# Chunk 0's norm ahead of the identity casts, its products on VectorE, zero rows written early, 128-wide weights in the state update, new planner constants

## The chip, the cores and the metric

One core of one Trainium2 chip runs the whole kernel in one launch. The metric is the device time in microseconds (us) of one execution; the figure of a kernel is the median of its runs. Engines are named as TensorE (PE in the profile, PEld for its weight loads), VectorE (DVE), ScalarE (ACT), GpSimd (POOL) and SyncE (SP, which issues most transfers).

## The reference

Three stages follow each other, in float32, on a batch of 4 and a sequence of 768:

```
k_n = k / (|k| + 1e-6)                            # 8 heads of 48
for t: y[t] = q[t] @ state
       state += beta[t] * outer(k_n[t], v[t] - k_n[t] @ state)
x = y as (4, 768, 384)
u = x + ((x^T @ U @ V)^T);  x1 = u + relu(u @ w_ch1) @ w_ch2      # 384 -> 1536 -> 384
u = x1 + real(fft2(x1));    un = layer norm of u over 384
out = u + relu(un @ w2_ch1) @ w2_ch2
```

## The kernel before

**Tiles and stages.** The attention is cut into 24 chunks of 128 tokens (unit `u`; 6 per batch). A chunk goes through `s_front` (L705: norms of k and q, products with beta and the norms, each value split into a high and a low fp16 part), `s_turn` (L740: transposes KT, BT, K2; for chunk 0 on TensorE with the fp16 identity `id16`, for the others by transposing transfers), `s_prep_a` (L811: G = products of these, masked on VectorE), `s_split` (L851: G into GPh and GPl), `s_prep_b` and `s_prep_c` (L885, L951: the inverse of a triangular matrix by blocks) and `s_solve` (L1037: the solve and the state update, chunk after chunk). `mix_chunk` (L1010) collects x^T U. The first MLP runs over 8 blocks of 384 tokens (`s_mlp`, L1166: L1190 is the first layer, L1196 its high part `hh`, L1209 its low part `hl`, L1226 the second layer); `s_mix` (L1255) makes its input, `s_out1` (L1341) its output `x1d`, one tensor of 769 rows in DRAM for each batch. Row 768 is a zero row. The second part (`second`, L1636) takes the FFT through tables: `fold` (L1415) loads rows of `x1d` into `xq`, gathers mirrored rows with indirect transfers (`gather`, L1458, indices in the tile `rows`), adds and subtracts them into `pm`, and splits that into `fs` for the matmuls. Then follow the layer norm (`s_in`) and the second MLP.

**Who sets the order.** Each engine runs its instructions in the order in which they were issued. That order is made while the program is built, by `Weave` (L62): every stage is a generator (a stream) that yields the cost of its next step on each engine that may take it, or a mark to wait for; `Weave.run` (L139) picks the step with the lowest start time plus bias. `PR0` holds the biases of the attention's streams until the first tile of the mix, `PRICE0` the factors with which `pick` (L97) weighs engines against each other, `AGE0` and `EPS0` the weight of a chunk's age, `FILL` how far a stream of weight conversions may run into the next step of an engine, `UP` and `UE` how many chunks take a variant in which TensorE adds with an identity matmul. These are times of the plan; on the chip an engine waits for what its instruction reads. The first weights (float64 words to float32, three VectorE passes per 128x384 piece, L293, L296 and L300) are converted beside the attention's chunks.

**What the change touches.** `attn_pools` (L535) loads k and q of chunk 0, the identity `id32`, and casts it three times on VectorE (L569, L571, L573) before any stream runs. `row_scales` (L641) squares k and q on ScalarE (L647, L653), sums on VectorE (L649) and calls `norm` (L662: square root L667, reciprocal L670). `s_front` multiplies (through the helper `tt`, L251) and splits (`sub`, L589). `s_solve` starts with a matmul on `ids` (L1046), and its state update multiplies with 64-wide parts of `kb16` (helper `hmm`, matmul at L1055). `fft_pools` (L1394) loads `rows` (L1401), clears row 96 of `xq` (L1405) and writes it as the zero row of each `x1d` (L1407) before the second part's streams run.

With `u < UE` `s_split` doesn't subtract on GpSimd: TensorE subtracts the high part from G in PSUM with the matrix `idm` (minus identity), and ScalarE copies the rest out:

```
if u < UE:
    yield {"p": 440}
    nc.tensor.matmul(g32..., self.idm, gs..., start=False, stop=True, ...)
    yield {"a": _a(512, True)}
    nc.scalar.activation(out=gl, in_=g32, func=ACTF.Copy)
else:
    yield from self.sub(gl, g32, gs, 512)
```

Of the kernel before, what the change touches and what calls it, by code (L numbers as in the profile page):

```python
# [21 lines left out]
DM = 384  # L22
# [9 lines left out]
NR = 3  # L32
NQ = 2
NV = 2
AGE0 = -5
AGE = 16
EPS0 = -1085
FILL = 47
EPS = -309
UP = 13  # L40
UE = 0
NP = 27
GATE = 3
UA = 8
SPARE = 270
SPW = 120
PR0 = (-337, -112, -95, -78, -360, -173, -425, 225)
PR = (-41, -98, -140, -142, 118, 51, -956, -408)
ME = -78
MX = -401  # L50
MB = -515
MB0 = -564
P2 = (-467, -323, -887, -360, -372, -386, -1140, -392)
MP = 39
HB = -550
WB1 = -575
WB = -15
PRICE0 = {'p': 1.0, 'v': 1.45, 'a': 0.71, 'g': 0.38}
PRICE = {'p': 1.0, 'v': 0.29, 'a': 0.22, 'g': 0.14}
PRICE2 = {'p': 1.0, 'v': 283.18, 'a': 3.3, 'g': 1.14}  # L60
SC = 16.0
# [152 lines left out]
class Builder:  # L214
# [39 lines left out]
    def setup(self):  # L254
        nc, tc, ctx = self.nc, self.tc, self.ctx
        self.cst = ctx.enter_context(tc.tile_pool(name="cst", bufs=1))
        self.psm = ctx.enter_context(tc.tile_pool(name="psm", bufs=1, space=PSUM))
        self.psu = ctx.enter_context(tc.tile_pool(name="psu", bufs=1, space=PSUM))
        self.acc = ctx.enter_context(tc.tile_pool(name="acc", bufs=1, space=PSUM))
        self.dr = ctx.enter_context(tc.tile_pool(name="dr", bufs=1, space=bass.MemoryType.DRAM))  # L260
        self.wts = ctx.enter_context(tc.tile_pool(name="wts", bufs=1))
        self.keep = ctx.enter_context(tc.tile_pool(name="keep", bufs=1))
        c = self.cst
        few = c.tile([128, 58], F32, name="few")
        at = 0
# [12 lines left out]
        self.Vst = c.tile([96, S], F32R, name="Vst")  # L278
        self.ones = c.tile([128, 128], F32, name="ones")
        nc.gpsimd.memset(self.ones, 1.0)  # L280
        self.fsc = some(2, B)
        self.wsc1, self.unscale1 = some(2), some(1)
        self.wtot1, self.wss1 = some(2), some(2)
        self.usq, self.ucc = some(2, KD), some(2, 9)
        self.fsq, self.ftot = some(2 * KD), some(1)
# [249 lines left out]
    def attn_pools(self, ctx):  # L535
# [30 lines left out]
            return ts  # L566

        self.id16 = self.ap1.tile([128, 128], F16, name="id16")
        nc.vector.tensor_copy(out=self.id16, in_=self.id32)  # L569
        self.ids = self.ap1.tile([128, 128], F16, name="ids")  # L570
        nc.vector.tensor_scalar(out=self.ids, in0=self.id32, scalar1=SC, scalar2=None, op0=ALU.mult)  # L571
        self.idm = self.ap1.tile([128, 128], F16, name="idm")
        nc.vector.tensor_scalar(out=self.idm, in0=self.id32, scalar1=-1.0, scalar2=None, op0=ALU.mult)  # L573

        self.kq16 = zeros(NQ, [128, 2, H, 2, 64], "kq16")
        self.kb16r = zeros(NK, [128, H, 2, 64], "kb16")
# [9 lines left out]
        e = yield {"v" if psum else "w": _v(n, 4 if half else 1 if psum else 2), "a": _a(n, psum)}, mode  # L586
        self.copy(e, out, in_)

    def sub(self, out, in0, in1, n, mode="chain", op=ALU.subtract):  # L589
        e = yield {"w": _v(n), "g": _g(n)}, mode  # L590
        self.tt(e, out, in0, in1, op)

    def s_scales(self):
# [47 lines left out]
    def row_scales(self, u, b, c, kq, sq):  # L641

        nc = self.nc
        n = H + 1
        ss = self.ap2.tile([128, n], F32, tag="ssq", name="ssq", bufs=1)
        yield {"a": _a(DM)}
        nc.scalar.activation(out=sq, in_=kq[:, 0], func=ACTF.Square)  # L647
        yield {"v": _v(DM)}, "par"
        nc.vector.tensor_reduce(out=ss[:, 0:H], in_=sq, op=ALU.add, axis=AX.X)  # L649
        yield {"a": _a(DM) + 187}, "par"  # L650
        if u < UE:
            sq = self.ap2.tile([128, 512], F32, tag="g32", name="g32")[:, 0:DM].rearrange("p (h d) -> p h d", h=H)
# [52 lines left out]
    def s_front(self):  # L705
# [3 lines left out]
        for u, (b, c) in self.each():  # L709
            yield ("kq", u)  # L710
            kq = self.kq.pop(u)
            kb = self.ap2.tile([128, H, D], F32, tag="kb", name="kb", bufs=1)
            rn, rb, rq, sq1 = yield from self.row_scales(u, b, c, kq, kb)
            kq16, kb16 = self.kq16[u % NQ], self.kb16r[u % NK]
            if u >= NQ:
                yield ("tk", u - NQ)
            e = yield {"g": 830, "w": _v(DM)}, "par"
            self.tt(e, kb, kq[:, 0], rb[:, :, None].to_broadcast(bc), ALU.mult)
            e = yield {"a": 507, "w": 330}, "par"
            if e == "a":  # L720
                nc.scalar.activation(out=kq16[:, 1, :, 0, 0:D], in_=kq[:, 1], func=ACTF.Copy, scale=rq)
            else:
                nc.vector.tensor_scalar(out=kq16[:, 1, :, 0, 0:D], in0=kq[:, 1], scalar1=rq, scalar2=None, op0=ALU.mult)
            e = yield {"g": 830, "w": _v(DM)}, "chain"
            self.tt(e, kq[:, 0], kq[:, 0], rn[:, :, None].to_broadcast(bc), ALU.mult)
            if u >= NK:
                yield ("sol", u - NK)
            yield from self.cp(kb16[:, :, 0, 0:D], kb, DM)
            yield from self.cp(kq16[:, 0, :, 0, 0:D], kq[:, 0], DM)
            yield "join"  # L730
            yield from self.sub(kb16[:, :, 1, 0:D], kb, kb16[:, :, 0, 0:D], DM, "par")
            yield from self.sub(kq16[:, 0, :, 1, 0:D], kq[:, 0], kq16[:, 0, :, 0, 0:D], DM, "par")
            yield {"w": _v(DM)}, "par"
            nc.vector.scalar_tensor_tensor(out=kq16[:, 1, :, 1, 0:D], in0=kq[:, 1], scalar=rq, in1=kq16[:, 1, :, 0, 0:D],
                                           op0=ALU.mult, op1=ALU.subtract)
# [4 lines left out]
    def s_turn(self):  # L740

        nc = self.nc
        for u, _ in self.each():
# [293 lines left out]
    def s_solve(self):  # L1037
# [5 lines left out]
        St = S32 = None  # L1043
        flat = "p h d -> p (h d)"
        R = self.psr.tile([128, H, D], F32, name="res")
        nc.tensor.matmul(R, self.ids, self.X128[:, :, 0:D], start=True, stop=True, skip_group_check=True)  # L1046

        def f16t(tag):
# [31 lines left out]
        for u, (b, c) in self.each():  # L1080
# [44 lines left out]
            terms.append((lambda h: GPh[:, h, 128:256], Ul))  # L1125
            if c < NC - 1:
                ps = work()
                yield from hmm(ps, [(lambda h: kb16[:, h, 0, :], Uh), (lambda h: kb16[:, h, 1, :], Uh),
                                    (lambda h: kb16[:, h, 0, :], Ul)], m=64)
                yield {"v": _v(n)}  # L1130
                if c == 0:
                    S32 = self.ap2.tile([64, H, D], F32, tag="S32", name="S32", bufs=1)
                    nc.vector.tensor_scalar(out=S32, in0=ps[0:64], scalar1=1.0 / SC, scalar2=None, op0=ALU.mult)
                else:
                    nc.vector.scalar_tensor_tensor(out=S32, in0=ps[0:64], scalar=1.0 / SC, in1=S32, op0=ALU.mult, op1=ALU.add)
# [14 lines left out]
    def attention(self):  # L1150
# [2 lines left out]
        streams = [self.s_solve(), self.s_prep_c(), self.s_prep_b(0), self.s_prep_a(), self.s_split(), self.s_front(), self.s_turn(),  # L1153
                   self.s_scales()]
        streams = self.att = [Stream(x, (y, y)) for x, y in zip(streams, PR0)]
        streams = streams + [Stream(self.s_prep_b(1), (PR0[2], PR0[2])), Stream(self.s_turned(), (PR0[6], PR0[6])), Stream(self.s_load(), (0.0, 0.0)), Stream(self.s_values(), (0.0, 0.0)), Stream(self.s_mixed(), (MX, MX))]
        peaks, weights = self.weight_parts(self.w11, self.w12)
        parts = self.mix_parts() + peaks + weights
        self.loads = len(parts)
# [95 lines left out]
    def s_mix(self):  # L1255
# [4 lines left out]
        for n in range(B * S // TB):  # L1260
# [30 lines left out]
                self.wv.post("hst", b)  # L1291
            if n >= 2:
                yield ("out", 0, n - 2)
            if n == 1:
                yield ("conv", self.loads - 1)
            ut = self.keep.tile([128, 2, KD, TB], F32, tag=f"uh{n % 2}", name="u1")
# [97 lines left out]
    def fft_pools(self, ctx):  # L1394
# [2 lines left out]
        self.fp1 = ctx.enter_context(tc.tile_pool(name="fp1", bufs=1))  # L1397
        self.fp2 = ctx.enter_context(tc.tile_pool(name="fp2", bufs=2))
        self.tab = {nm: self.fp1.tile([128, 2, 2, w], F16, name=nm) for nm, w in TABS}
        self.rows = self.fp1.tile([128, KD * B + 4], mybir.dt.int32, name="rows")  # L1400
        nc.sync.dma_start(self.rows, self.crows)  # L1401
        self.xq = [self.fp1.tile([97, 4, DM], F32, name=f"xq{i}") for i in range(2)]
        for i, x in enumerate(self.xq):
            if i == 0:
                nc.gpsimd.memset(x[96:97], 0.0)  # L1405
                for x1 in self.x1d:
                    nc.sync.dma_start(x1[S:S + 1], x[96:97, 3, :])  # L1407

    def s_tables(self):
        for (nm, w), src in zip(TABS, self.ctab):  # L1410
# [4 lines left out]
    def fold(self, b):  # L1415
# [5 lines left out]
        for i, x in enumerate(self.xq):  # L1421
# [8 lines left out]
            for y in range(2):  # L1430
                yield from self.gather(b, x[0:96, 1 + y, :], KD * B + 2 * i + y)
            yield "join"
            pm = self.fp1.tile([97, 2, 2, 2 * NE], F32, tag="pm", name="pm")
            for y, op in enumerate((ALU.add, ALU.subtract)):
                e = yield {"w": _v(2 * DM), "g": _g(2 * DM)}, "par"
# [317 lines left out]
```

## Time and profile before

| | us |
|---|---|
| median of 3 runs | 1038.92 (1038.15 to 1038.94) |
| the profiled execution | 1041.91 |
| its span, first to last instruction | 1039.8 |
| TensorE busy | 913.1 (88%) |
| VectorE busy | 724.9 (70%) |
| ScalarE busy | 548.6 (53%) |
| GpSimd busy | 352.2 (34%) |
| mean granted TensorE clock | 0.939 of full speed |

The profile is of one execution. Busy times of an engine add up its instructions; a stage is read from its own stretch, since the attention (to about 575 us), the first MLP (from 211 us) and the second part (from 577 us) overlap and have different limits. A line of the timeline gives start, duration, engine, source line, what it writes and reads, and in brackets the idle time before it with what ended that.

### The profile page before, as it was taken

To read this page: it belongs to the slowest core of one execution; us is meant where nothing else is said; L and a number is where in the kernel's file an instruction comes from. 1 tells how busy PE (TensorE), PEld (TensorE's weight loads), DVE (VectorE), ACT (ScalarE), POOL (GpSimd) and SP (SyncE) were. 2 spreads that over 40 slices of the span, in tenths; PEclk is the share of its full clock that TensorE was granted. 3 is DMA by queue.
4 is the path that set the end of the run, shared out by engine and by line. 5 is a ranking of instruction groups with operands and counts; after the bars stand their busy time and mean duration, and the time that the engine had idled before them with its cause. 6 is when DMAs were issued, how large, how long until landed. Compare 5 with 4: busy or idle time off the path is not lost. (4 is left out here: it accounts for less than half of the span.)

```text
span 1039.8 us, 25511 instructions
## 1 busy us (share of the span) xinstructions
PE 913.1 (88%) x10282; PEld 622.6 (60%) x10282; DVE 724.9 (70%) x1664; ACT 548.6 (53%) x1358; POOL 352.2 (34%) x330
## 2 busy tenths in 40 slices
PE   3465777589999899999999879999999999999998
PEld 2344665356777666676676546655756665655655
DVE  6898889898898998998765367765735554444532
ACT  5665676767777766667655244447723232222221
POOL 3554244213444323454110360046555532012010
PEclk8575989589999999999999989999999999999999
DMA  6996677316756565543502546522211311202110
GB/s 189 224 219 163 160 183 174 78 39 146 152 133 162 105 151 112 142 109 79 114 25 70 164 105 192 130 87 71 35 54 50 95 28 54 69 24 61 58 34 23
DMA packets 158253, 110.87 MB, mean 107 GB/s; under 512 B 117484, under 2 KB 146424, under 8 KB 158136
## 3 DMA queue, kind: packets, MB, share of 16 engines
q1 hardware_dynamic: 155688, 102.01, 40.6%
q0 software_dynamic: 2448, 7.24, 2.5%
q8 instruction: 80, 1.31, 0.5%
q14 instruction: 37, 0.30, 0.1%
HBM read 55.63 MB, written 14.16 MB: 67 GB/s over the span
## 5 line engine op out<-in xcount | busy, mean ns | idle before, releaser
L1226 PE MATMUL acc<-w2s,hh 128*128 128x384 f16 x1152 | 281.8, 326 | 4.9 <-DVE u L1624 3.1
L1190 PEld LDWEIGHTS <-w1s 128*128 128x128 f16 x1728 | 163.5, 98 | 114.5 <-issue 14.7
L1196 ACT ACTIVATE hh<-ps_h 128x384 f16<-128x384 f32 x192 | 93.7, 488 | 205.6 <-PE ps_h L1190 201.8
L251 POOL TENSOR_TENSOR GPl<-g,GPh 128x512 f16<-128x512 f32 x92 | 116.1, 1262 | 235.1 <-ACT GPh L244 174.2
L1209 DVE SCALAR_TENSOR_TENSOR hl<-ps_h,hh 128x384 f16<-128x384 f32 x147 | 81.6, 555 | 161.6 <-ACT hh L1196 155.8
L1226 PE MATMUL acc<-w2s,hl 128*128 128x384 f16 x576 | 188.1, 327 | 0.2 <-DVE hl L1209 0.2
L1190 PE MATMUL ps_h<-u,w1s 128*128 128x384 f16 x864 | 169.6, 329 | 11.9 <-DVE hl L1209 10.5
L1190 PE MATMUL ps_h<-uh,w1s 128*128 128x384 f16 x864 | 157.9, 327 | 0.0
L1226 PEld LDWEIGHTS <-hh 128*128 128x128 f16 x1152 | 106.2, 98 | 64.8 <-issue 8.0
L902 PEld LDWEIGHTS <-bd 128*128 128x128 f16 x1728 | 71.6, 99 | 45.7 <-issue 18.6
L1226 PEld LDWEIGHTS <-hl 128*128 128x128 f16 x576 | 56.2, 98 | 38.2 <-DVE hl L1209 0.6
L841 DVE TENSOR_TENSOR g<-ps_g,mask 128x512 f32<-128x512 f32 x96 | 65.6, 683 | 12.1 <-PE ps_g L835 11.0
L834 PE MATMUL ps_g<-KT,BT 128*128 128x256 f16 x192 | 54.0, 301 | 10.0 <-ACT t L993 5.0
L244 ACT ACTIVATE GPh<-g 128x512 f16<-128x512 f32 x75 | 47.0, 626 | 28.0 <-DVE g L841 27.3
L251 POOL TENSOR_TENSOR pair<-x1f,pair 128x384 f16<-128x384 f32 x24 | 22.2, 925 | 111.8 <-ACT pair L1594 106.8
L251 POOL TENSOR_TENSOR pm<-xq 97x768 f32<-97x768 f32 (+1 forms) x16 | 29.3, 1850 | 79.5 <-DMA xq<-x1d 72.1
L835 PE MATMUL ps_g<-K,BT 128*128 128x256 f16 x192 | 54.6, 305 | 1.9 <-DMA K<-KT 1.8
L1068 ACT ACTIVATE rh<-res 128x384 f16<-128x384 f32 x63 | 30.5, 484 | 20.0 <-PE res L1055 10.2
L902 PE MATMUL lanes<-R,bd 128*128 128x32 f16 x768 | 34.7, 179 | 4.5 <-ACT R L244 2.9
L882 DVE TENSOR_TENSOR bd<-Xc,mmask 128x1024 f16<-128x1024 f16 x48 | 34.2, 712 | 5.9 <-ACT Xc L936 5.5
L1055 PEld LDWEIGHTS <-GPh 128*128 128x128 f16 x768 | 30.2, 98 | 9.7 <-issue 6.7
L251 POOL TENSOR_TENSOR kb<-kq,rb 128x384 f32<-128x384 f32 x21 | 18.2, 867 | 50.8 <-DVE rb L658 10.9
(270 smaller groups left out, 1866.6 us busy)
## 6 DMA issues: line engine op xcount, KB each, us to landing
wst<-in_moe_w_ch_dram SPq DMA_DIRECT2D x51, 384.0 KB, 3.4
K<-KT SPq DMA_DIRECT2D x46, 256.0 KB, 3.9
kq<-in_k_dram SPq DMA_DIRECT2D x24, 192.0 KB, 3.8
kq<-in_q_dram SPq DMA_DIRECT2D x24, 192.0 KB, 4.2
vt<-in_v_dram SPq DMA_DIRECT2D x24, 192.0 KB, 2.9
xnd<-vt SPq DMA_DIRECT2D x24, 192.0 KB, 3.5
xn<-xnd SPq DMA_DIRECT2D x24, 192.0 KB, 3.0
x1d<-u SPq DMA_DIRECT2D x24, 192.0 KB, 1.9
```

The lines of the kernel that those rows point to most:

```text
L244: self.nc.scalar.activation(out=out, in_=in_, func=ACTF.Copy)
L251: (self.nc.vector if eng == "v" else self.nc.gpsimd).tensor_tensor(out=out, in0=in0, in1=in1, op=op)
L834: nc.tensor.matmul(o, BT[:, h, :], KT[:, :, h, :], start=i == 0, stop=False, skip_group_check=True)
L835: nc.tensor.matmul(o, BT[:, h, :], K2[:, :, h, :], start=False, stop=True, skip_group_check=True)
L841: nc.vector.tensor_tensor(out=g32.rearrange("p i (a t) -> p (i a) t", a=2), in0=ps.rearrange("p i (a t) -> p (i a) t", a=2), in1=self.mask ...
L882: self.nc.vector.tensor_tensor(out=dst.rearrange("p h (j c) -> p h j c", j=n), in0=x, in1=mask[:, None, :, :].to_broadcast(shape), op=ALU. ...
L902: nc.tensor.matmul(ps[:, h, :], lhs[:, h, :], rhs[:, h, :], start=plus is None, stop=plus is None or h == H - 1)
L1068: nc.scalar.activation(out=t, in_=R, func=ACTF.Copy, scale=-1.0 / SC)
L1190: nc.tensor.matmul(ps[:, i, :], w[:, k, fs], u[x][:, k, :], start=(m == 0), stop=(m == 3 * KD - 1))
L1196: nc.scalar.activation(out=hh, in_=ps, func=ACTF.Relu, scale=1.0 if wi else 1.0 - 2.0 ** -11)
L1209: nc.vector.scalar_tensor_tensor(out=hl, in0=ps, scalar=0.0, in1=hh, op0=ALU.max, op1=ALU.subtract)
L1226: nc.tensor.matmul(acc, h[:, ds_], w, start=(f == 0 and j == 0), stop=(f == KF - 1 and j == 2))
```

## The change

Three casts of the identity become a stream, `s_unit`, that waits until chunk 0's norm is done; the solve and chunk 0's transposes wait for it. Chunk 0's two products and two splits may run on VectorE alone, and the second square of chunk 0 is written to a block of `bd[3]` (of the next chunks, below `UE`, to a `g32` tile). The row table and a 12x32 zero tile are placed in the pool that lives from the start; the table's load and the four zero-row writes are issued in `s_mix` at n = 2. In the state update the weights are 128 wide (but for the last one), so that rows 64 to 127 of the product's tile receive values that nothing reads. A mark `gd` with offset `GD` = 0 is waited for before `pm`. The planner's constants of the first part change.

```diff
-AGE0 = -5
+AGE0 = 6
+GD = 0.0
-EPS0 = -1085
-FILL = 47
+EPS0 = -1190
+FILL = 148
-UP = 13
-UE = 0
+UP = 11
+UE = 4
-PR0 = (-337, -112, -95, -78, -360, -173, -425, 225)
+PR0 = (-226, -196, -174, -118, -335, -164, -241, 81)
-MB0 = -564
+MB0 = -441
-WB = -15
-PRICE0 = {'p': 1.0, 'v': 1.45, 'a': 0.71, 'g': 0.38}
+WB = -18
+PRICE0 = {'p': 1.0, 'v': 1.45, 'a': 0.24, 'g': 0.14}
...
+        self.rows = c.tile([128, KD * B + 4], mybir.dt.int32, name="rows")
+        self.zero = c.tile([12, 32], F32, name="zero")
+        nc.gpsimd.memset(self.zero, 0.0)
...
-        nc.vector.tensor_copy(out=self.id16, in_=self.id32)
-        nc.vector.tensor_scalar(out=self.ids, in0=self.id32, scalar1=SC, ...)
-        nc.vector.tensor_scalar(out=self.idm, in0=self.id32, scalar1=-1.0, ...)
...
-        if u < UE:
+        if u == 0:
+            sq = self.bd[3].rearrange(...).bitcast(F32)[:, 0:DM].rearrange(...)
+        elif u < UE:
...
             rn, rb, rq, sq1 = yield from self.row_scales(u, b, c, kq, kb)
+            if u == 0:
+                self.wv.post("scaled")
-            e = yield {"g": 830, "w": _v(DM)}, "par"
+            e = yield {"g": 830, "w": _v(DM)} if u else {"w": _v(DM)}, "par"
             self.tt(e, kb, kq[:, 0], rb[:, :, None].to_broadcast(bc), ALU.mult)
...
-            e = yield {"g": 830, "w": _v(DM)}, "chain"
+            e = yield {"g": 830, "w": _v(DM)} if u else {"w": _v(DM)}, "chain"
             self.tt(e, kq[:, 0], kq[:, 0], rn[:, :, None].to_broadcast(bc), ALU.mult)
...
+            yield from self.sub(kb16[:, :, 1, 0:D], kb, kb16[:, :, 0, 0:D], DM, "par", fast=u == 0)
+            yield from self.sub(kq16[:, 0, :, 1, 0:D], kq[:, 0], kq16[:, 0, :, 0, 0:D], DM, "par", fast=u == 0)
...
             if u == 0:
+                yield ("unit",)
...
+    def s_unit(self):
+        yield ("scaled",)
+        for t, x in ((self.id16, 1.0), (self.ids, SC), (self.idm, -1.0)):
+            yield {"v": 210.0}, "par"
+            self.nc.vector.tensor_scalar(out=t, in0=self.id32, scalar1=x, scalar2=None, op0=ALU.mult)
+        self.wv.post("unit")
...
         R = self.psr.tile([128, H, D], F32, name="res")
+        yield ("unit",)
         nc.tensor.matmul(R, self.ids, self.X128[:, :, 0:D], ...)
...
-                yield from hmm(ps, [(lambda h: kb16[:, h, 0, :], Uh), (lambda h: kb16[:, h, 1, :], Uh),
-                                    (lambda h: kb16[:, h, 0, :], Ul)], m=64)
+                yield self.pe(3 * H, 48, 64)
+                kf = kb16.rearrange("p h s d -> p (h s d)")
+                for i, (y, x) in enumerate(((0, Uh), (1, Uh), (0, Ul))):
+                    for h in range(H):
+                        z = 64 * (2 * h + y)
+                        z1 = min(z + 128, 128 * H)
+                        nc.tensor.matmul(ps[0:z1 - z, h, :], kf[:, z:z1], x[:, h, :], ...)
...
+            if n == 2:
+                self.nc.sync.dma_start(self.rows, self.crows)
+                for x1 in self.x1d:
+                    self.nc.sync.dma_start(x1[S:S + 1].rearrange("o (a c) -> (o a) c", a=12), self.zero)
...
-        self.rows = self.fp1.tile([128, KD * B + 4], mybir.dt.int32, name="rows")
-        nc.sync.dma_start(self.rows, self.crows)
...
-                for x1 in self.x1d:
-                    nc.sync.dma_start(x1[S:S + 1], x[96:97, 3, :])
...
+            self.wv.post("gd", b, i)
+            self.wv.mark["gd", b, i] += GD
+            yield ("gd", b, i)
             pm = self.fp1.tile([97, 2, 2, 2 * NE], F32, tag="pm", name="pm")
```

## Rows read from the trace of the kernel before

**Rows 1.** Busy time by stretch: engines (instructions), granted clock, DMA share, GB/s.

```profile
core 0: us, PE busy (x) PEld busy (x) DVE busy (x) ACT busy (x) POOL busy (x), PEclk, DMA share, GB/s
...
20.00:40.00 20.00, 8.97 (x82) 5.49 (x80) 18.20 (x42) 10.83 (x29) 11.57 (x12) 0.51 0.88 228
...
120.00:200.00 80.00, 52.02 (x965) 41.55 (x964) 69.47 (x160) 55.94 (x139) 32.96 (x32) 0.84 0.67 157
...
300.00:400.00 100.00, 95.53 (x1514) 70.08 (x1513) 91.47 (x206) 71.31 (x186) 37.57 (x34) 1.00 0.56 130
...
800.00:900.00 100.00, 99.07 (x682) 63.98 (x681) 52.92 (x137) 29.51 (x69) 32.11 (x30) 1.00 0.22 62
```

**Rows 2.** Timeline of TensorE: the first matmuls of the first MLP.

```profile
210.80 1.13 PE L1190 MATMUL ps_h<-u,w1s 128*128 128x384 f16 x3
```

**Rows 3.** Waits of TensorE, 560 to 1040 us: total us, times, longest us.

```profile
PE ps_h L1190 <- DVE hl L1209: 10.5, 4, 8.1
```

**Rows 4.** Timeline of single engines from 577 us (start, us), and a piece of the chain.

```profile
579.12 1.14 SPq L1407 DMA_DIRECT2D x1d<-xq  x4
...
583.43 1.14 POOL L1461 DMA_INDIRECT xq<-x1d,rows  x1 [4.66 <-DMA xq<-x1d]
...
585.43 0.43 SPq L1412 DMA_DIRECT2D sd<-in_sd_dram  x1
...
592.50 3.71 POOL L251 TENSOR_TENSOR pm<-xq 97x768 f32<-97x768 f32 x2 [6.71 <-DMA xq<-x1d]
...
600.49 0.94 ACT L1451 ACTIVATE fs<-pm,few 97x772 f16<-97x772 f32 x1 [8.96 <-POOL pm L251]
...
603.48 3.04 PE L1190 MATMUL ps_h<-u,w1s 128*128 128x384 f16 x9 [8.15 <-DVE hl L1209]
...
608.44 1.46 PE ps_h L1190 x9
...
757.25 0.91 POOL L1461 DMA_INDIRECT xq<-x1d,rows  x1 [0.30 <-issue]
761.21 3.59 POOL L251 TENSOR_TENSOR pm<-xq 97x768 f32<-97x768 f32 x2 [3.05 <-issue]
```

**Rows 5.** Timeline, 5 to 14 us: chunk 0's norm, products, splits and transposes.

```profile
5.42 0.21 ACT L675 ACTIVATE n_h<-n_s 128x9 f32<-128x9 f32 x1
6.73 0.23 DVE L569 CAST id<-id 128x128 f16<-128x128 f32 x1 [2.33 <-DMA id<-in_cident_dram]
...
7.15 0.21 DVE L670 RECIPROCAL n_t<-n_s 128x9 f32<-128x9 f32 x1
...
8.45 0.82 POOL L251 TENSOR_TENSOR kb<-kq,rb 128x384 f32<-128x384 f32 x1 [5.62 <-DMA wst<-in_moe_V_dram]
...
11.80 1.25 POOL L251 TENSOR_TENSOR kq<-kq,kq 128x384 f16<-128x384 f32 x1
...
13.11 1.03 PE L767 MATMUL ps_t<-id,kq 128*128 128x128 f16 x8 [5.45 <-POOL kq L251]
```

**Rows 6.** Groups by line, 0 to 125 us: busy us, mean ns | idle before.

```profile
L841 DVE TENSOR_TENSOR g<-ps_g,mask 128x512 f32<-128x512 f32 x22 | 15.0, 683 | 2.7 <-PE ps_g L835 2.3 <-POOL GPl L251 0.2
...
L293 DVE TENSOR_SCALAR wfp<-wst 128x384 uint32<-128x384 uint32 (+2 forms) x23 | 12.5, 545 | 1.3 <-DMA wst<-in_moe_U_dram 0.6 <-ACT UU L328 0.4
...
L244 ACT ACTIVATE GPh<-g 128x512 f16<-128x512 f32 x21 | 13.1, 626 | 9.8 <-DVE g L841 9.8
...
L251 POOL TENSOR_TENSOR GPl<-g,GPh 128x512 f16<-128x512 f32 x21 | 25.0, 1192 | 14.5 <-ACT GPh L244 14.4
```

**Rows 7.** Timeline of TensorE, 62 to 65 us: the state update and the output of chunk 0.

```profile
62.55 0.66 PE L1055 MATMUL ps_s<-Uh,kb 128*64 128x48 f16 x16 [0.53 <-DVE Ul L1121]
63.05 0.41 PE L1055 MATMUL ps_s<-Ul,kb 128*64 128x48 f16 x8
...
64.10 0.36 PE L1055 MATMUL ps_s<-Uh,GPh 128*128 128x48 f16 x8
64.31 0.36 PE L1055 MATMUL ps_s<-Uh,GPl 128*128 128x48 f16 x8
```

More of the change, by code (lines that the diff above doesn't have):

```diff
@@ L34 @@
 NV = 2
-AGE0 = -5
+AGE0 = 6
 AGE = 16
-EPS0 = -1085
-FILL = 47
+GD = 0.0
+TUNE = ("GD",)
+EPS0 = -1190
+FILL = 148
 EPS = -309
-UP = 13
-UE = 0
+UP = 11
+UE = 4
 NP = 27
@@ L568, in attn_pools @@
         self.id16 = self.ap1.tile([128, 128], F16, name="id16")
-        nc.vector.tensor_copy(out=self.id16, in_=self.id32)
         self.ids = self.ap1.tile([128, 128], F16, name="ids")
-        nc.vector.tensor_scalar(out=self.ids, in0=self.id32, scalar1=SC, scalar2=None, op0=ALU.mult)
         self.idm = self.ap1.tile([128, 128], F16, name="idm")
-        nc.vector.tensor_scalar(out=self.idm, in0=self.id32, scalar1=-1.0, scalar2=None, op0=ALU.mult)
         self.kq16 = zeros(NQ, [128, 2, H, 2, 64], "kq16")
@@ L587, in cp, with sub @@
         self.copy(e, out, in_)
-    def sub(self, out, in0, in1, n, mode="chain", op=ALU.subtract):
-        e = yield {"w": _v(n), "g": _g(n)}, mode
+    def sub(self, out, in0, in1, n, mode="chain", op=ALU.subtract, fast=False):
+        e = yield {"w": _v(n)} if fast else {"w": _v(n), "g": _g(n)}, mode
         self.tt(e, out, in0, in1, op)
@@ L650, in row_scales @@
         yield {"a": _a(DM) + 187}, "par"
-        if u < UE:
+        if u == 0:
+            sq = self.bd[3].rearrange("p h c -> p (h c)").bitcast(F32)[:, 0:DM].rearrange("p (h d) -> p h d", h=H)
+        elif u < UE:
             sq = self.ap2.tile([128, 512], F32, tag="g32", name="g32")[:, 0:DM].rearrange("p (h d) -> p h d", h=H)
@@ L730, in s_front @@
             yield "join"
-            yield from self.sub(kb16[:, :, 1, 0:D], kb, kb16[:, :, 0, 0:D], DM, "par")
-            yield from self.sub(kq16[:, 0, :, 1, 0:D], kq[:, 0], kq16[:, 0, :, 0, 0:D], DM, "par")
+            yield from self.sub(kb16[:, :, 1, 0:D], kb, kb16[:, :, 0, 0:D], DM, "par", fast=u == 0)
+            yield from self.sub(kq16[:, 0, :, 1, 0:D], kq[:, 0], kq16[:, 0, :, 0, 0:D], DM, "par", fast=u == 0)
             yield {"w": _v(DM)}, "par"
@@ L1127, in s_solve @@
                 ps = work()
-                yield from hmm(ps, [(lambda h: kb16[:, h, 0, :], Uh), (lambda h: kb16[:, h, 1, :], Uh),
-                                    (lambda h: kb16[:, h, 0, :], Ul)], m=64)
+                yield self.pe(3 * H, 48, 64)
[4 more added lines that the diff above has]
+                        z1 = min(z + 128, 128 * H)
+                        nc.tensor.matmul(ps[0:z1 - z, h, :], kf[:, z:z1], x[:, h, :], start=i == 0 and h == 0,
+                                         stop=i == 2 and h == H - 1, skip_group_check=True)
                 yield {"v": _v(n)}
@@ L1155, in attention @@
         streams = self.att = [Stream(x, (y, y)) for x, y in zip(streams, PR0)]
-        streams = streams + [Stream(self.s_prep_b(1), (PR0[2], PR0[2])), Stream(self.s_turned(), (PR0[6], PR0[6])), Stream(self.s_load(), (0.0, 0.0)), Stream(self.s_values(), (0.0, 0.0)), Stream(self.s_mixed(), (MX, MX))]
+        streams = streams + [Stream(self.s_prep_b(1), (PR0[2], PR0[2])), Stream(self.s_turned(), (PR0[6], PR0[6])), Stream(self.s_unit(), (0.0, 0.0)), Stream(self.s_load(), (0.0, 0.0)), Stream(self.s_values(), (0.0, 0.0)), Stream(self.s_mixed(), (MX, MX))]
         peaks, weights = self.weight_parts(self.w11, self.w12)
```

## The prediction

> **What bounds the kernel now.** I read the busy time by stage first, then what TensorE waited for late in the span, then the order of time at the two places that the change touches. The stages [rows 1] show two regimes. From 20 to 200 us TensorE is busy well under 70% of the time while VectorE is at 91% (18.20 of 20) and 87% (69.47 of 80), the transfers take 0.88 of the DMA engines at first, and the granted clock is 0.51 at first, which is the 1.2 GHz level for nearly all of that stretch. From about 300 us TensorE is the bound: 95.53 of 100 us, later 99.07 of 100, at a clock of 1.00. The first matmul of the first MLP stands at 210.80 us [rows 2]. So a microsecond counts in three ways: the dense regime beginning earlier, TensorE doing less in it, and a hole in it closing.
>
> The only large hole late in the span is one wait: of four waits of the first MLP layer for `hl` that sum to 10.5 us, one takes 8.1 us [rows 3]. Its cause is in [rows 4]. The fold of batch 0 (the start of the second part) gathers rows of `x1d` with indirect transfers on GpSimd. The first gather starts at 583.43, after GpSimd stood idle for 4.66 us behind a transfer. The row puts that down to a load of `xq`, but the gather doesn't touch what that load writes; it does read the tensor into which four writes of zero rows were issued on SyncE from 579.12 on, and I take those as the cause. `pm` on GpSimd starts only at 592.50; ScalarE's `fs`, queued ahead of the MLP's `hh`, waits 8.96 us for it until 600.49; then VectorE's `fs`, then `hl`; TensorE resumes at 603.48 after 8.15 us. Its first nine matmuls take 3.04 us where nine take 1.46 a little later, twice as long, as at the low one of the two clocks.
>
> **The change part by part.** Durations are of the profiled execution (1041.91 us, span 1039.8), which is 2.99 us above the median of the runs, 1038.92. Savings are taken off the median.
>
> 1. *Fold: zero rows and row table written in the first part.* Removed ahead of the fold: one load of the row table and four tiny writes on SyncE, and the gather's wait for them. GpSimd was free at 583.43 - 4.66 = 578.77, so two gathers can be out by 578.77 + 2 x 0.91 and the gap between, say 581.2, instead of 592.50 - 6.71 = 585.79. In a later fold the second gather ends at 757.25 + 0.91 = 758.16 and `pm` starts at 761.21, 3.05 us on [rows 4]; here it took 6.71 because loads of the FFT tables were issued up to 585.43 + 0.43 among them. So `pm` starts between 584.3 and 587.9, 8.2 to 4.6 us earlier. `hl` must still wait for its own conversions in VectorE's queue, so some stall stays. I take 5.5 us of the 8.15. Lower end 0 (the gathers still land behind the tables); upper end 8.15 + (3.04 - 1.46) = 9.7 us, if the clock never falls. What is late next is ScalarE's `fs` against `hh`, by a smaller amount. The five DMAs now issue in the first part at n = 2 of the mix stage, on SyncE, ahead of that tile's later transposes. I cost them at nothing: the writes of before took SyncE 1.14 us, and in that part of the run VectorE and TensorE set the pace, not the queue; uncovered it is about 1.2 us once. The new planner mark before `pm` adds no instruction: 0.
>
> 2. *Chunk 0's opening.* ScalarE's last result for the norm was under way at 5.42, but VectorE stood at the identity's cast, which waited 2.33 us for the load and ran at 6.73; the norm's reciprocal came at 7.15 [rows 5]. Moved behind the norm: 7.15 - 5.42 = 1.7 us. The two products and two splits took GpSimd from 8.45 to 11.80 + 1.25 = 13.05, passes of 0.82 to 1.25 us; a 128x384 pass on VectorE takes 0.55 [rows 6], so four take 2.2 and, with ScalarE's casts between, about 2.9: 1.7 us less. Against this the three casts (6.73 to 7.15, 0.42 us) now stand in VectorE's queue ahead of splits or converted weights, and VectorE takes over 2.2 us. Who waits: the transposes, which need the cast identity and began at 13.11 behind GpSimd's last split. Net 1.7 + 1.7 - 0.4 = 3.0 us at that point. But the stage behind it has VectorE at 91% and DMA at 0.88, so not all of it arrives at 210.8: I take 2.0, ends 0 and 3.4. The first square's own scratch removes a wait on ScalarE, yet the same reduction still feeds the square root: 0, at most one 0.55 us pass.
>
> 3. *State update with 128-wide weights.* The rows of the solve [rows 7] give the step: 16 products with 64-wide `kb` take 63.05 - 62.55 = 0.50 us, 31 ns each; 8 with 128-wide `GPh` take 64.31 - 64.10 = 0.21 us, 26 ns each. 23 of a chunk's 24 become 128 wide: 23 x 5 = 0.12 us; 20 chunks have one: 2.4 us, of which 15 chunks (1.8 us) lie after 210.8. The extra output rows are not read.
>
> 4. *UE 0 to 4, UP 13 to 11.* For four chunks the low part of G (16 of the 1192 ns passes on GpSimd [rows 6]) becomes an identity matmul and a ScalarE copy in PSUM. TensorE has room there [rows 1]; the new cost is a wait in its queue for VectorE's mask and ScalarE's copy, 683 + 626 ns a pair. Covered by other chunks' matmuls: 0; uncovered, 16 x 1.31 = 21 us. For two chunks eight 256-column matmuls leave TensorE, and a VectorE sum takes the place of a copy. A 384-column matmul takes 1.46 / 9 = 0.16 us, so at most 8 x 0.16 = 1.3 us gained; VectorE takes on at most 8 x 0.55 us, in a stage where it is at 91% and TensorE at 96%. I take 0.2, and 2.0 for parts 3 and 4 together (ends 0 and 3.7).
>
> 5. *Planner constants* (prices, biases, ages, FILL 47 to 148) move order in the first 200 us and remove no instruction. No row shows the new order. FILL lets a weight conversion start up to 101 ns later into another engine step's slot; up to 125 us there are 23 x 3 such passes [rows 6], so at worst 69 x 0.101 = 7.0 us of delay; a gain can't be excluded either. I take 0.
>
> Sum: 5.5 + 2.0 + 2.0 = 9.5; 1038.9 - 9.5 = 1029.4, call it 1029.5 (of the profiled execution: 1032.4).
>
> **A rule that speaks against part 3.** The rows show the 128-wide weights at the shorter step. The Trainium skill, page TensorE: Matmul & The Clock Gate, section LDWEIGHTS, makes a load's time the number of columns over 1.2 (in ns), whatever the rows: an estimate by it is 53 ns for 64 columns and 107 for 128, and by it alone part 3 would cost 23 x 20 x 53 ns = 25 us rather than save 2.4. The trace disagrees for this type and shape: I go by its 26 against 31 ns.
>
> **The rivals.**
> - *A, the fold doesn't gain.* The gathers still land with the table loads, which also move up, and `pm` starts where it did. For it: 6.71 us from issue to `pm`. Against it: 4.66 us of GpSimd's wait has a named cause that goes. Only parts 2 to 4 remain: 1038.9 - 4.0 = 1034.9.
> - *B, the new order eats the gain.* Conversions squeezed ahead of the attention chain delay 210.8 by the full 7.0 us and swallow part 2: 1038.9 - 7.5 + 7.0 = 1038.4, no change. For it: VectorE at 91%. Against it: only passes on the chain count.
> - *C, slower: TensorE's queue in the first four chunks.* The identity matmuls wait in order for mask and copy, and the solve of these chunks comes later. Place: 20 to 120 us; price up to 21 us; it decides once more than 7.5 + 2.1 = 9.6 us of it stays uncovered. With two thirds, 14 us: 1038.9 - 7.5 + 14 = 1045.4. Against it: two banks alternate, and TensorE works only 8.97 of 20 us there.
> - *D, slower: wider weights load longer.* If the step grew with the columns, 31 ns more for 23 x 20 products is 14.3 us: 1038.9 - 7.5 + 14.3 = 1045.7. Against it: [rows 7]. By that rule of the Trainium skill's page, this is what would happen.
>
> **How the numbers follow.** Forecast 0.60, A 0.17, B 0.10, C 0.10, D 0.03. A measurement here can tell about 0.2%, 2.1 us. Faster holds forecast and A, 0.77; within 0.2% is B, 0.10; slower is C and D, 0.13. Low end: all upper ends at once, 9.7 + 3.4 + 3.7 = 16.8, give 1022.1; a gain by order may stand in for one of them, and 1 us is left for it: 1021. The high end takes in A and B with some of B's spread: 1040. Outside are C and D and a little at the bottom, under 2 in 10.
>
> **What would show it.** Right: the first gather within 1 us of GpSimd coming free and no transfer ahead of it; `pm` 4.6 us or more earlier against the end of attention; the 8.1 us wait under 3; the reciprocal under 6 us and the first transposes near 10; `kb` loads 128 wide at 26 ns; the first MLP matmul near 208. Wrong: that matmul later than 211, identity matmuls of `idm` with idle TensorE before them in the first 100 us, or `pm` again 9 us after the first gather, as now (592.50 - 583.43).

## The result and the profile after

The changed kernel takes 1027.22 us (median of 4 runs, 1024.69 to 1028.83) against 1038.54 us of the kernel before in the same session: a ratio of 0.9889, 95% interval 0.9873 to 0.9906, 11.5 us faster (9.8 to 13.2). The forecast was 1029.5. The two profiled executions lie 17.2 us apart (1041.91 and 1024.69), further than the medians: what two single profiles show is read for its place and cause, and sizes are taken from the medians and ratios.

Head of the page after:

```profile
span 1022.9 us, 25488 instructions
...
PE 914.5 (89%) x10293; PEld 623.0 (61%) x10293; DVE 716.4 (70%) x1650; ACT 562.7 (55%) x1391; POOL 330.4 (32%) x311
```

Busy time by stretch after, columns as in [rows 1]:

```profile
20.00:40.00 20.00, 10.78 (x110) 6.62 (x108) 17.56 (x41) 13.54 (x34) 7.10 (x8) 0.50 0.84 180
...
120.00:200.00 80.00, 55.04 (x957) 44.59 (x957) 70.35 (x157) 58.37 (x150) 29.33 (x27) 0.78 0.69 160
...
300.00:400.00 100.00, 91.06 (x1409) 65.13 (x1407) 85.12 (x191) 72.32 (x188) 37.72 (x33) 1.00 0.59 134
...
800.00:900.00 100.00, 99.27 (x654) 62.30 (x653) 49.47 (x134) 27.73 (x64) 25.49 (x25) 1.00 0.21 58
```

Against [rows 1] work has gone from GpSimd (11.57 to 7.10 us of the first stretch) to ScalarE (10.83 to 13.54) and TensorE (8.97 to 10.78). VectorE is as full as before, and the granted clock of the first stretch is still the 1.2 GHz level, 0.50. Up to 200 us TensorE has run 2119 matmuls, 1914 before, and so has less left from 300 us; the gain lies before 120 us, for from 120 to 200 us it runs 957 against 965, and its longer busy time there (55.04 us against 52.02) goes with a lower clock (0.78 against 0.84).

Timeline after, the opening and the first matmul of the first MLP (start, duration, engine, line):

```profile
3.73 0.52 ACT L657 ACTIVATE bd<-kq 128x384 f32<-128x384 f32 x1
...
4.77 0.21 DVE L674 RECIPROCAL n_t<-n_s 128x9 f32<-128x9 f32 x1 [0.43 <-ACT n_s L671]
...
7.09 0.17 DVE L662 TENSOR_TENSOR rb<-n_r,betaT 128x8 f32<-128x8 f32 x1 [1.36 <-DMA betaT<-in_beta_dram]
...
7.77 0.22 DVE L804 TENSOR_SCALAR id<-id 128x128 f16<-128x128 f32 x1
...
9.38 0.55 DVE L253 TENSOR_TENSOR kq<-kq,kq 128x384 f16<-128x384 f32 x1
...
9.99 1.03 PE L774 MATMUL ps_t<-id,kq 128*128 128x128 f16 x8 [0.84 <-DVE kq L253]
...
204.90 1.14 PE L1212 MATMUL ps_h<-u,w1s 128*128 128x384 f16 x3
```

The second square of the norm in the kernel before:

```profile
4.43 0.52 ACT L653 ACTIVATE kb<-kq 128x384 f32<-128x384 f32 x1 [0.62 <-DVE ssq L649]
```

With a scratch of its own the square doesn't wait for the sum on VectorE and starts 0.7 us earlier. The reciprocal stands 2.4 us and the transposes 3.1 us earlier than in [rows 5]. Part of the 3.1 is chance: in the six kernels below that keep the casts ahead of the norm and GpSimd's passes the transposes start between 11.92 and 12.46 us, not at 13.11, so some 2 us is the better figure. VectorE now waits 1.36 us for the load of beta, which I had not foreseen: in the kernel before that load had landed by the time the identity's wait was over. The first MLP starts 5.9 us earlier than in [rows 2].

Timeline after, the last output of the attention's solve and the fold of batch 0, and then TensorE's wait for `hl` from 540 us (total, times, longest):

```profile
566.46 0.58 ACT L1164 ACTIVATE vt<-ps_s,dn 128x384 f32<-128x384 f32 x1 [1.00 <-PE ps_s L1071]
...
571.18 1.02 POOL L1486 DMA_INDIRECT xq<-x1d,rows  x1 [0.16 <-issue]
...
575.87 0.33 SPq L1434 DMA_DIRECT2D sd<-in_sd_dram  x1
...
578.32 3.59 POOL L253 TENSOR_TENSOR pm<-xq 97x768 f32<-97x768 f32 x2 [4.89 <-DMA xq<-x1d,rows]
...
586.21 0.94 ACT L1476 ACTIVATE fs<-pm,few 97x772 f16<-97x772 f32 x1 [3.14 <-POOL pm L253]
```

```profile
PE ps_h L1212 <- DVE hl L1231: 3.0, 2, 2.3
```

The same output of the solve in the kernel before:

```profile
574.21 0.58 ACT L1142 ACTIVATE vt<-ps_s,dn 128x384 f32<-128x384 f32 x1 [0.52 <-PE ps_s L1055]
```

The gather waits for nothing (0.16 us of issue against 4.66 in [rows 4]); the longest wait of [rows 3] falls from 8.1 to 2.3 us. In the kernel before the hole was followed by a stretch at a lower clock; after it there is none. Busy time by stretch at that place, before and then after (the granted clock is the first figure behind the five engines):

```profile
604.00:610.00 6.00, 6.00 (x28) 3.17 (x27) 4.09 (x7) 2.73 (x9) 2.87 (x2) 0.72 0.62 188
```

```profile
580.00:590.00 10.00, 7.67 (x48) 4.50 (x46) 5.55 (x9) 3.31 (x9) 8.93 (x8) 1.00 0.31 98
```

### The profile page after: what moved, and what is told of

The parts are those of the page before. It is cut to its first block, busy times and chain, and to the rows that moved or that the text cites. A ratio compares the mean times of both kernels' runs of the same rounds, so it can differ in the third digit from the quotient of the medians.

```text
span 1022.9 us, 25488 instructions
## 1 busy us (share of the span) xinstructions
PE 914.5 (89%) x10293; PEld 623.0 (61%) x10293; DVE 716.4 (70%) x1650; ACT 562.7 (55%) x1391; POOL 330.4 (32%) x311
## 5 line engine op out<-in xcount | busy, mean ns | idle before, releaser
L253 POOL TENSOR_TENSOR GPl<-g,GPh 128x512 f16<-128x512 f32 x78 | 97.4, 1249 | 177.5 <-ACT GPh L246 137.9
L856 DVE TENSOR_TENSOR g<-ps_g,mask 128x512 f32<-128x512 f32 x80 | 54.5, 681 | 9.9 <-PE ps_g L850 7.9
L246 ACT ACTIVATE GPh<-g 128x512 f16<-128x512 f32 x66 | 41.3, 626 | 16.1 <-DVE g L856 15.4
L253 POOL TENSOR_TENSOR kb<-kq,rb 128x384 f32<-128x384 f32 x17 | 14.9, 876 | 106.9 <-DVE rb L662 53.6
L897 DVE TENSOR_TENSOR bd<-Xc,mmask 128x1024 f16<-128x1024 f16 x48 | 37.8, 790 | 6.6 <-ACT Xc L951 6.1
```

The lines of the kernel that those rows point to most:

```text
L246: self.nc.scalar.activation(out=out, in_=in_, func=ACTF.Copy)
L253: (self.nc.vector if eng == "v" else self.nc.gpsimd).tensor_tensor(out=out, in0=in0, in1=in1, op=op)
L856: nc.vector.tensor_tensor(out=g32.rearrange("p i (a t) -> p (i a) t", a=2), in0=ps.rearrange("p i (a t) -> p (i a) t", a=2), in1=self.mask ...
L897: self.nc.vector.tensor_tensor(out=dst.rearrange("p h (j c) -> p h j c", j=n), in0=x, in1=mask[:, None, :, :].to_broadcast(shape), op=ALU. ...
```

## The experiments

The theory at the start was that of the prediction: each part brings its own gain, and the gains add up. The rival was that part of the gain belongs to the order in which the planner puts the instructions, and to no part alone. Every ratio is to runs of the kernel before in the same session. "Order unchanged" means that the other instructions stand in the same sequence on every engine.

| run | ratio, 95% interval | to before, us |
|---|---|---|
| before + early rows | 0.9948 (0.9929 to 0.9967) | -5.4 |
| before + zero rows alone | 0.9941 (0.9917 to 0.9965) | -6.1 |
| before + wide weights | 0.9995 (0.9976 to 1.0014) | -0.5 |
| before + opening, replanned | 1.0272 (1.0246 to 1.0298) | +28.2 |
| before + opening, order unchanged | 1.0001 (0.9986 to 1.0016) | +0.1 |
| before + constants, UE and UP | 1.0098 (1.0076 to 1.0120) | +10.2 |
| after, old constants, UE and UP | 1.0246 (1.0219 to 1.0274) | +25.5 |
| after, old opening, replanned | 1.0068 (1.0042 to 1.0095) | +7.1 |
| after, late rows | 0.9935 (0.9917 to 0.9953) | -6.7 |
| after, old opening, order unchanged | 0.9895 (0.9873 to 0.9916) | -10.9 |
| after, GpSimd's split in four chunks | 0.9925 (0.9895 to 0.9955) | -7.8 |
| after, narrow weights | 0.9878 (0.9855 to 0.9901) | -12.7 |
| after | 0.9889 (0.9873 to 0.9906) | -11.5 |

**The rows written early: alone, and taken back (order unchanged in both).**

```diff
+            if n == 2:
+                self.nc.sync.dma_start(self.rows, self.crows)
+                for x1 in self.x1d:
+                    self.nc.sync.dma_start(x1[S:S + 1].rearrange(...), self.zero)
...
-        nc.sync.dma_start(self.rows, self.crows)
...
-                    nc.sync.dma_start(x1[S:S + 1], x[96:97, 3, :])
```

> The kernel before with only the row table and the zero rows moved into the first part. Theory M (each part pays for itself): the first gather starts within 1 us of GpSimd coming free, the TensorE wait of 8.1 us falls to 1 to 3 us, 1038.5 - 5.5 to 8 = 1030.5 to 1033. Theory O (the new constants' order does nearly all of it): the gathers still land among the table loads, the wait stays over 6 us, 1036.5 to 1039.

> The changed kernel with the row table and the zero rows written at the start of the second part, as before; no other instruction changes its place. Theory M (the fold's wait has its own price): 4 to 8 us more, 1031 to 1035, with one wait of TensorE for hl of 6 us or more behind attention's end. Rival: with the new order the fold is hidden anyway, 1027 to 1029.

Alone 5.4 us (3.4 to 7.4). Taken back from the changed kernel, 0.9935 - 0.9889 = 0.0046, 4.8 us, give or take 2.5 (the two half-widths added in squares, as in all such differences below). So the part is worth about 5 us in either order, as theory M of both runs has it. Its mark `gd` moves no instruction. Fold of the kernel with it alone, then the `hl` wait of the changed kernel without it:

```profile
578.42 1.01 POOL L1464 DMA_INDIRECT xq<-x1d,rows  x1 [0.16 <-issue]
...
584.85 3.92 POOL L251 TENSOR_TENSOR pm<-xq 97x768 f32<-97x768 f32 x2 [4.19 <-DMA xq<-x1d,rows]
```

```profile
PE ps_h L1208 <- DVE hl L1227: 7.3, 2, 6.8
```

**The zero rows alone** (the row table stays where it was):

```diff
+            if n == 2:
+                for x1 in self.x1d:
+                    self.nc.sync.dma_start(x1[S:S + 1].rearrange(...), self.zero)
...
-                    nc.sync.dma_start(x1[S:S + 1], x[96:97, 3, :])
```

> The kernel before with only the zero rows of the two scratch tables written early, from a small tile; the row table is still loaded where it was, at the start of the second part. If the zero rows' writes are what the first gather waited for, it now waits for the row table at most, the product on GpSimd comes within 2 us of where it stood with both moved, and the time is 1032 to 1034.5 us. If the row table's load is the longer of the two waits, the gather still starts some 4 us after GpSimd came free and the time is 1036 to 1038 us.

```profile
575.77 0.90 SPq L1429 DMA_DIRECT2D xq<-x1d  x2
...
576.21 1.01 POOL L1464 DMA_INDIRECT xq<-x1d,rows  x1 [0.27 <-DMA rows<-in_crows_dram]
...
582.57 3.92 POOL L251 TENSOR_TENSOR pm<-xq 97x768 f32<-97x768 f32 x2 [4.13 <-DMA xq<-x1d,rows]
```

The table's load now ends the gather's wait, and that wait is 0.27 us. The whole gain is there without moving the table: the 4.66 us of [rows 4] were the zero rows' writes, though the row named a load of `xq`. That the gather waits for such a load instead is out: here it starts 0.44 us after the first of these loads was issued and before the second was through the queue.

**128-wide weights: alone, and taken back (order unchanged in both).**

```diff
-                yield from hmm(ps, [(lambda h: kb16[:, h, 0, :], Uh), ...], m=64)
+                        z1 = min(z + 128, 128 * H)
+                        nc.tensor.matmul(ps[0:z1 - z, h, :], kf[:, z:z1], x[:, h, :], ...)
```

> The kernel before with only the 128-wide weights in the state update; rows 64 to 127 of the product tile hold values that nothing reads. Theory M: a step of 26 ns in place of 31, 1.8 to 2.4 us less: 1036 to 1037. Theory O: the loads were hidden beside other work, no change within 1 us. If a load's time grew with its columns: 1050 or more.

> The changed kernel with the 64-wide weight loads of the multiplied keys again, at the new order to the instruction otherwise. Theory, as at the old order the width is worth nothing (within 1.5 us of the changed kernel, 1026 to 1028.5 us). Rival, TensorE is more nearly full in the new order's attention, so the 12 loads less and 2.4 us of TensorE show: 1029 to 1030 us.

Nothing that the runs can tell in either order: -0.5 us (-2.5 to 1.5) alone, and 0.0011 the other way, 1.1 us give or take 2.9, taken back. The two together, weighted by their errors, give 0.0 us, give or take 1.6: the 2.4 us of TensorE don't reach the end, while a gain of 1 us may. (The "12 loads less" of the second expectation is a slip: both kernels load `kb` 480 times.) The timeline of one chunk tells what TensorE gains. Before, from the matmul ahead of the group to the one behind it:

```profile
347.86 0.32 PE L1226 MATMUL acc<-w2s,hl 128*128 128x384 f16 x1
348.12 0.69 PE L1055 MATMUL ps_s<-Uh,kb 128*64 128x48 f16 x16
348.64 0.41 PE L1055 MATMUL ps_s<-Ul,kb 128*64 128x48 f16 x8
348.99 0.36 PE L902 MATMUL lanes<-R,bd 128*128 128x32 f16 x8
```

The same chunk with only the wide weights, and the line's groups by shape in the changed kernel, 300 to 480 us (count, busy us, mean ns):

```profile
345.22 0.32 PE L1232 MATMUL acc<-w2s,hl 128*128 128x384 f16 x1
345.38 0.68 PE L1134 MATMUL ps_s<-Uh,kb 128*128 128x48 f16 x16
345.99 0.37 PE L1134 MATMUL ps_s<-Ul,kb 128*128 128x48 f16 x8
346.20 0.35 PE L902 MATMUL lanes<-R,bd 128*128 128x32 f16 x8
```

```profile
L1150 PE MATMUL ps_s<-Uh,kb 128*128 128x48 f16 x90 | 3.2, 183 | 0.4 <-DVE Ul L1137 0.4
...
L1150 PE MATMUL ps_s<-Uh,kb 128*64 128x48 f16 x6 | 1.3, 210 | 0.0
```

The last eight step at (346.20 - 345.99) / 8 = 26 ns, as predicted. But among the first sixteen stands the one load that stayed 64 wide, and each of these alone keeps TensorE busy 1.3 / 6 = 0.22 us: the sixteen take 0.61 us to the next ones, where 64-wide ones take 0.52. In the kernel before, every matmul of the group is narrow, and the change of width lies at its ends: from the matmul ahead of it to its first one it takes 0.26 us, 0.16 with wide weights, and its last eight take 0.35 us to the next instruction, not 8 x 31 ns = 0.25. In all the stretch takes 1.13 us before and 0.98 with wide weights. Added up from the traces over the 20 chunks, with the order unchanged, TensorE is through such stretches 1.2 us sooner in the old order and 1.8 us in the new one, of the 2.4. That the width next door matters is seen where the matmul right ahead of or behind the group is itself 64 wide (six chunks of the old order): there the wide group saves nothing or takes up to 0.16 us longer. The Trainium skill, page TensorEngine Tiling (Array Packing), section Key Properties, says that a change of the tiling mode drains TensorE; if a change of width is one, these rows agree, at some 0.1 us at an end of the group and 0.2 us for the lone load. A version in which the last load is padded to 128 columns was not tried.

**The opening: alone, replanned and with the order unchanged.**

```diff
-        nc.vector.tensor_copy(out=self.id16, in_=self.id32)
...
+            e = yield {"g": 830, "w": _v(DM)} if u else {"w": _v(DM)}, "par"
...
+            yield from self.sub(..., fast=u == 0)
...
+    def s_unit(self):
```

> The kernel before with only chunk 0's opening changed (casts behind the norm, its products and splits on VectorE, own scratch). Theory M: the first transposes 3 us earlier at 10.1 us, of which 2 us reach the first MLP matmul: 1036 to 1037. Theory O: the 3 us are gone before 211 us, as VectorE and the transfers bound that stretch: 1038 to 1039.

Neither theory foresaw this: it starts 3 us earlier and ends 28 us later. Its transposes, its waits of TensorE from 540 us, and two of its stretches:

```profile
10.15 1.04 PE L769 MATMUL ps_t<-id,kq 128*128 128x128 f16 x8 [0.44 <-DVE kq L251]
```

```profile
PE ps_h L1201 <- DMA uh<-pair: 5.8, 1, 5.8
PE acc L1237 <- DVE u L1368: 5.4, 3, 4.3
```

```profile
200.00:300.00 100.00, 81.57 (x1174) 56.84 (x1174) 84.28 (x176) 70.24 (x172) 25.62 (x24) 0.90 0.42 88
...
700.00:800.00 100.00, 88.42 (x574) 55.15 (x572) 49.84 (x111) 50.78 (x113) 61.08 (x59) 0.95 0.21 61
```

The same stretches of the kernel before:

```profile
200.00:300.00 100.00, 89.76 (x1374) 65.54 (x1374) 88.49 (x190) 74.86 (x192) 33.72 (x29) 0.93 0.54 116
...
700.00:800.00 100.00, 95.13 (x627) 60.22 (x626) 53.38 (x122) 50.18 (x112) 61.78 (x59) 0.98 0.22 56
```

The new streams make the planner lay the first part out differently: TensorE loses 8.2 us of work from 200 to 300 us and 6.7 from 700 to 800, where the second MLP takes over from the first and waits for its transposed input (`uh`, at 743 us). Neither place has to do with chunk 0. So I made the opening's work without showing it to the planner:

```diff
-        self.tt(e, out, in0, in1, op)
+        self.tt("v" if fast else e, out, in0, in1, op)
...
+            if u == 0:
+                for t, x in ((self.id16, 1.0), (self.ids, SC), (self.idm, -1.0)):
+                    nc.vector.tensor_scalar(out=t, in0=self.id32, scalar1=x, ...)
```

> The kernel before with chunk 0's opening changed but hidden from the planner: VectorE does the casts behind the norm and the four passes, while the planner still counts the old steps, so all other instructions keep their order on every engine. Theory P (the 28 us that the opening cost alone came from the planner's new order, not from the work): the first transposes near 10 us as in that run, and the time 1 to 3 us under the kernel before, 1034.5 to 1036.5. Theory W (VectorE's added 2.2 us and the later casts themselves hold up the attention): 1045 or more.

```profile
4.76 0.22 DVE L669 RECIPROCAL n_t<-n_s 128x9 f32<-128x9 f32 x1 [0.43 <-ACT n_s L666]
...
8.04 0.36 DVE L293 TENSOR_SCALAR wfp<-wst 128x192 uint32<-128x192 uint32 x1 [0.52 <-DMA wst<-in_moe_U_dram]
8.31 0.55 DVE L251 TENSOR_TENSOR kb<-kq,rb 128x384 f32<-128x384 f32 x1
...
12.52 1.03 PE L770 MATMUL ps_t<-id,kq 128*128 128x128 f16 x8 [4.58 <-DVE kq L251]
```

The early reciprocal runs into VectorE's queue: in the old order six passes of the weight conversions, the first of which waits for a load, stand ahead of and between the products and splits. The transposes come out at 12.52 us, no earlier than with the old opening, and the time doesn't move. So theory W is out and the 28 us are the order's, as theory P has it, but P's early transposes and its gain of 1 to 3 us did not come, and what early transposes are worth in the old order was not measured. And the other way round, the changed kernel with the old opening at the new order:

```diff
-        self.tt(e, out, in0, in1, op)
+        self.tt("g" if fast else e, out, in0, in1, op)
...
-        if u == 0:
-            sq = self.bd[3]...
```

> The changed kernel with chunk 0's opening done the old way (three casts of the identity before the streams start, the four passes of chunk 0's norm and products on GpSimd, the old scratch for its second square), while every other instruction on every queue stays where the new order has it (TensorE's order is the same to the instruction). Theory, the opening's work has a price of its own once the order lets its result through: first transposes 2 to 3 us later than 9.99 us, first product matmul near 18 to 19 us, and the time 2 to 4 us above the changed kernel, 1029 to 1031 us. Rival, only the order counts: the delay is taken up by slack before the first MLP's stage, whose first matmul stays within 1 us of 204.9, and the time is 1026 to 1028 us.

```profile
12.24 1.03 PE L775 MATMUL ps_t<-id,kq 128*128 128x128 f16 x8 [4.96 <-POOL kq L253]
...
208.62 0.81 PE L1212 MATMUL ps_h<-u,w1s 128*128 128x384 f16 x2
```

The transposes are 2.25 us later and the first MLP 3.7, against what the rival wanted, but the median says 0.9895 - 0.9889 = 0.0006, 0.6 us give or take 2.8, below what the theory wanted. What the earlier opening is worth at the end stays open between nothing and some 3 us.

**The constants with UE and UP: alone, and taken back; and the whole opening taken back, replanned.**

```diff
-EPS0 = -1085
-FILL = 47
+EPS0 = -1190
+FILL = 148
-UP = 13
-UE = 0
+UP = 11
+UE = 4
...
```

> The kernel before with only the planner's constants changed, UE and UP among them. Theory M: the order moves the first MLP matmul by no more than 4 us either way: 1034.5 to 1042.5, most likely 1037. Theory O: the first MLP matmul comes 5 us or more earlier and the end with it: 1033 or less.

> The changed kernel with the planner's constants of before (UE and UP too), everything else kept. Theory P (constants and streams fit each other; either without the other costs): the opening's 28 us loss comes back, less the fold's 5: 1055 to 1063. Theory A (the parts add up): the constants cost 11 us alone, so taking them out gives 1027 - 11 = 1016.

> The changed kernel with chunk 0's opening as before, everything else kept. Theory P: the new constants without the new opening lose as they did alone, 1048.5 less the fold's 5 and the weights' 0 to 2: 1041 to 1045. Theory A: the opening cost 28 us alone, so 1027 - 28 = 999.

These refute the adding up: 1064.12 and 1045.11 us against the 1016 and 999 of theory A, and just above the ranges of theory P. The constants with UE and UP cost 10.2 us alone, which both theories of that run missed, the opening 28.2; together with the rest they are part of a gain of 11.5. Without the constants, UE and UP the changed kernel loses 0.0357, 37 us; without the opening's streams 0.0179, 19 us. All four bad orders have one wait of TensorE for `uh` between 715 and 745 us, of 5.8 or 6.0 us, which neither the kernel before nor the changed one has. That of the constants alone, and its busy time in that stretch:

```profile
PE ps_h L1190 <- DMA uh<-pair: 5.8, 1, 5.8
```

```profile
700.00:800.00 100.00, 84.76 (x549) 52.65 (x548) 51.94 (x114) 42.01 (x93) 58.70 (x56) 0.95 0.20 58
```

TensorE does 10.4 us less there than in the kernel before (95.13), although the first MLP starts at 208.75 us, 2 us earlier than in [rows 2]. The wait is a part of each loss; the rest was not followed up.

**GpSimd's split in the first four chunks again, at the new order.**

```diff
-        elif u < UE:
-            sq = self.ap2.tile([128, 512], F32, tag="g32", name="g32")...
...
-                early = u < UE
+                early = False
...
-                    nc.tensor.matmul(g32..., self.idm, gs..., start=False, stop=True, ...)
...
-                    nc.scalar.activation(out=gl, in_=g32, func=ACTF.Copy)
+                    nc.gpsimd.tensor_tensor(out=gl, in0=g32, in1=gs, op=ALU.subtract)
```

> The changed kernel with the remainder of the first four chunks' splits taken by GpSimd's subtraction again, in place of the matmul against the negated identity and ScalarE's copy, at an order that is otherwise the new one. Theory, this part is a small gain: 0 to 4 us slower without it, 1027 to 1031 us. Rival, the prediction's case C in a weak form (TensorE's queue stands behind the new matmuls): without them it is 1025 us or less.

0.9925 - 0.9889 = 0.0036: 3.7 us slower without the identity matmuls, give or take 3.5, just clear of nothing, and one of a dozen comparisons. Waits of TensorE up to 205 us and the first MLP, of this kernel, and then the waits of the changed one:

```profile
PE lanes L914 <- DVE bd L894: 9.8, 7, 4.6
```

```profile
209.57 1.13 PE L1209 MATMUL ps_h<-u,w1s 128*128 128x384 f16 x3
```

```profile
PE ps_g L883 <- ACT GPh L876: 5.0, 7, 1.4
PE ps_g L849 <- ACT GPl L885: 4.0, 6, 1.0
...
PE lanes L917 <- DVE bd L897: 3.5, 7, 1.0
```

The identity matmuls do wait (5.0 us for the high part, 4.0 us behind them for the copy), but in the kernel with GpSimd's passes TensorE waits longer for `bd` (9.8 us against 3.5, of it 8.6 from 20 to 60 us), a tile that this edit leaves as it is, and the first MLP starts 4.7 us later. What holds up `bd` there was not followed up, and a small part of the edit goes beside the question: chunks 1 to 3 square into the shared scratch again.

## Why the prediction was right, and where it was not

The total was right within 2.3 us, and no rival came about. Step by step the sum was less good than its total, and that the misses nearly cancel (too much for parts 2 and 3, too little for part 4 and the order) is luck:

- **Part 1, 5.5 us: right**, cause included. It measured 5.4 and 6.1 us in the old order and 4.8 in the new one. `pm` after the last output of the attention's solve comes 578.32 - 566.46 = 11.9 us on, against 592.50 - 574.21 = 18.3 in the profile before: 6.4 us, within the 4.6 to 8.2; in the old order it comes 11.1 and 11.2 us on with early rows and with zero rows alone. The stretch at the lower clock went, as the upper end had it. Rival A is out.
- **Part 2, 2.0 us: the place was right, the price too high.** Reciprocal and transposes came where they were forecast, but some 2 of the 3.0 us are the change's, and partly by other terms than the sum's. The square's own scratch, put at nothing, brought 0.7 us of the reciprocal's 2.4, and the wait of 1.36 us for beta, which takes that and more back, stands in no term. The "2.0" measured a gain of -0.1 us (1.6 either way) in the old order, where VectorE's queue gave it back, and 0.6 us (2.8 either way) in the new one. The step that failed is the share that was to arrive.
- **Part 3, 2.4 us of TensorE: mis-sized.** 1.2 us in the old order and 1.8 in the new by the traces, and 0.0 us (1.6 either way) at the end. The step of 26 against 31 ns was right; multiplying it by 23 left out what changes of width cost: the lone 64-wide load takes 0.22 us a chunk, more than the shorter steps bring, and what is left comes from the ends of the group, which the sum didn't count. Rival D is out.
- **Part 4, 0.2 us: mis-sized the other way**, at 3.7 us (3.5 either way) for UE. I priced what TensorE's queue would wait (rival C: 9.0 of the 21 us bound are there, and the sign that was to show the prediction wrong, idle TensorE before matmuls on `idm` in the first 100 us, did show: seven of the sixteen, all before 75 us) and gave no price to the 16 GpSimd passes that go from the chunks' chain.
- **Part 5, 0 us: a term that doesn't stand alone.** Its bound from FILL, 7.0 us of delay, was far too small: the constants with UE and UP cost 10.2 us by themselves, and the opening's streams without them 28.2. The prediction took the order for a term beside the others, while it decides whether the others arrive; and it looked for the price of the order before 210.8 us, while part of it lies beyond 700 us.

What was shown: the fold's part pays about 5 us in both orders, and its cause is the zero rows' writes; the wide weights pay nothing that the runs can tell; the new streams and the new constants are each a loss without the other. What was only added up: taken back one by one from the changed kernel, rows, UE, opening and width give 4.8 + 3.7 + 0.6 - 1.1 = 8.0 of its 11.5 us. The other 3.5, with an error of some 7 us, would be the order itself and UP. A kernel with the new order and none of the parts was not run, so whether the order has a gain of its own stays open. No run beat the changed kernel by more than the runs can tell; the one with narrow weights equals it.

## What to carry to other kernels

A tiny write that a gather depends on belongs in an earlier stage: four rows of zeros cost 5 us here, and the row that showed the wait named another transfer. Where a planner sets the order, a part's gain is tested with the order held still, and planner constants and steps are judged only together, since a step that is 2 to 3 us better locally cost 28 us under constants made for another set of steps. When matmuls of one width replace those of another, look at the odd one that is left and at the neighbours: one in the middle cost 0.22 us a chunk, where the shorter steps of the other 23 bring 23 x 5 ns = 0.12.

## What the runs showed of the hardware that was not expected

- One 64-wide load among 128-wide ones keeps TensorE busy 0.22 us alone, eight times the 26 ns step of its neighbours; a group of 64-wide ones between 128-wide ones pays some 0.1 us at each end, and none at an end where the neighbour is 64 wide too.
- The 8.15 us without matmuls in [rows 4] was followed by 6 us at a granted clock of 0.72; with TensorE 7.67 of 10 us busy at the same place the clock stayed at 1.00.
